# An attention and gated-MLP kernel on one core: identity made on the chip, shorter loads, and conversion steps given to GpSimd

## The chip, the cores and the metric

The kernel runs on 1 core of a Trainium2 chip. The metric is device time in microseconds (us), from the first to the last work of one execution. One execution was also recorded by the hardware profiler; views of that record are called the profile, or the trace where single instructions are meant.

A core has five engines that run side by side, each through its own instructions in a fixed order: PE (TensorE, matrix products), ACT (ScalarE), DVE (VectorE), POOL (GpSimd) and SP (SyncE, which here only issues DMA transfers). They wait for each other through semaphores. An engine whose next instruction waits does nothing else meanwhile.

## The reference, cut to what matters

```python
def phi(x):                       # x: batch 4, heads 4, 1088 positions, 32 channels
    a = np.einsum('rd,bhsd->bhsr', S1, x)        # r = 8
    b = np.einsum('rd,bhsd->bhsr', S2, x)
    return np.einsum('bhsi,bhsj->bhsij', a, b).reshape(*x.shape[:-1], 64)
q_p, k_p = phi(q), phi(k)
kv = np.einsum('bhsf,bhsd->bhfd', k_p, v)
num = np.einsum('bhsf,bhfd->bhsd', q_p, kv)
den = np.einsum('bhsf,bhf->bhs', q_p, k_p.sum(2))[..., None] + 1e-06
x = (num / den).transpose(0, 2, 1, 3).reshape(4, 1088, 128)

h = np.maximum(x @ w_in, 0.0)                    # 128 -> 1024
u, v = h[..., :512], h[..., 512:]
v_n = (v - mean(v)) / np.sqrt(var(v) + 1e-06)    # over the 512 channels
v_s = np.einsum('ts,bsd->btd', w_spatial, v_n) + b_spatial[None, :, None]
out = (u * v_s) @ w_out                          # 512 -> 128
```

`S1`, `S2`, `w_in` and `w_out` come in double precision (64 bits), the rest in single precision.

## The kernel before, in words

**Products.** Most products are made in three: each operand is split into a high part (ACT rounds it to the matmul's fast format) and a low part (what is left, a subtraction on DVE or POOL), and high x high, high x low and low x high are added up in PSUM (`mm3`, `high`, `low`). `wTh`/`wTl` are the two parts of `w_spatial`, `vh`/`vl` those of the normalised `v`, `wih`/`wil` and `woh`/`wol` those of `w_in` and `w_out`.

**Stages.** Batch 0 goes through `attention0`: keys and values of three groups of 384 positions are projected (`project`), expanded (`features`, tile `kp`), summed into `kv`, masked into `kd0` by a table of ones and zeros, then the queries of the three groups are expanded, transposed against an identity matrix `ident_sb`, multiplied (`sums`), divided, and transposed again into `xh`/`xl`. `hidden_v` makes the `v` half of the hidden layer in nine tiles of 128 positions, with the statistics of each row on DVE (`bn_stats`). `main` runs the spatial product. For batch 0 its first 424 columns are done for all four blocks of channels at once: first a high phase (36 pairs of matmuls against `wTh`, nine row tiles `kt` in order), then a low phase (36 matmuls against `wTl`). In between, `hidden` makes `u` (tile `pu`). Then follow the remaining columns, and the same for batches 1 to 3, whose attention is laid beside the main loop of the batch before. 

**Weights.** `w_in` is loaded in two halves (`load_wi`; half 1 serves `hidden_v`, half 0 serves `u`), `w_out` in one. Each is turned from 64 bits into 32 by `from_f64`: seven steps over 512 columns (absolute value, clamp, shift, sign, exponent, two more to add the lower word) and then the split. The small table `sk` (`S1`, `S2`) goes through the same steps over 64 columns, and nothing can be projected before it is ready. `load_w` loads `w_spatial` in 27 pieces (nine `kt`, three column ranges: `W0`, `W1`, `W2`).

**What sets the order.** `Order` holds every operation with its inputs, its outputs and an assumed cost, and `schedule` writes one order for each engine ahead of time, from tables of numbers: `LEADS`, `T_MAIN`, `PACE`, `STRETCH`, `SLACK`, `LEAD`, `FIRST`, and `FORCE`, which says which engines may take an operation. Where it expects PE to stand idle in the first 50 us it puts in short matmuls of no use (`fill`, L431), beside eight at the start (L427). On the chip each engine keeps its written order, whatever the real times are. In the kernel before, `FORCE` keeps the low parts `W0` and `W1` and the low parts of `v` of batch 0 (`vl0`) on DVE; all steps of `from_f64` but the absolute value are on DVE too.

**Loads.** All DMAs are issued by SP in order. `ident_sb` is loaded from the input `idn`: the identity in 128 columns, and two masks in 6 columns. A tile of the tag `pl` (8 buffers), `kt` or `v` (3 each) can be loaded again only after its last reader is done.

Of the kernel before, what the change touches and what calls it, by code (L numbers as in the profile page):

```python
# [9 lines left out]
F32 = mybir.dt.float32  # L10
# [4 lines left out]
ALU = mybir.AluOpType  # L15
# [4 lines left out]
P = 128  # L20
# [26 lines left out]
T_MAIN = (39.0, 143.0, 197.0, 292.0)  # L47
PACE = (1.145, 0.898, 1.306, 1.037)
STRETCH = 1.64
FORCE = {'abs': ['ACT'], 'norm0': ['ACT', 'DVE'], 'vl0': ['DVE'], 'v90': ['ACT'], 'W0': ['DVE'], 'W1': ['DVE'], 'W2': ['POOL']}  # L50

FIRST = ('wt21', 'wt20', 'wt02', 'wt12', 'wt11', 'wt40', 'wt01', 'wt22')
# [18 lines left out]
FIRST_RATE, LOW_DELAY = 0.18, 4.4  # L71
# [48 lines left out]
class Order:  # L120
# [13 lines left out]
    def op(self, eng, cost, fn, r=(), w=(), due=None, kb=0, alts=(), sh=False, kind=None, after=0.0, lead=0.0, f4=False):  # L134
# [208 lines left out]

def c_dve(n):
    return 152 + 1.045 * n


def c_dve2(n, ptr=False):
    return (270 if ptr else 155) + 0.53 * n


def c_pool(n):
    return 90 + 2.4 * n


def c_mm(n, k=1):
    return k * max((n + 11.8) / 2.25, 111)


@with_exitstack  # L360
def tile_kernel(ctx: ExitStack, tc: tile.TileContext, kT, qT, vA, sks, idn, wT, w_in, w_out, bsp, out):

# [85 lines left out]
    def from_f64(x32, raw, n):  # L448

        def w(i):
            return raw[:, :2 * n].bitcast(U32).rearrange("p (n w) -> p w n", w=2)[:, i]

        def x():
            return x32[:, :n]

        def xb():
            return x32[:, :n].bitcast(U32)

        def step(cost, f, r, w):
            op("DVE", cost, lambda: f(nc.vector), r=r, w=w, sh=True)

        c2, c1 = c_dve2(n), c_dve(n)

        if n > NSK:
            op("ACT", c_act(n), lambda: nc.scalar.activation(x(), w(1).bitcast(F32), AF.Abs), r=[raw], w=[(x32, "x")], sh=True, alts=[("DVE", c2, lambda: nc.vector.tensor_scalar(out=xb(), in0=w(1), scalar1=0x7FFFFFFF, scalar2=None, op0=ALU.bitwise_and))], kind="abs")
        else:
            step(c2, lambda v: v.tensor_scalar(out=xb(), in0=w(1), scalar1=0x7FFFFFFF, scalar2=None, op0=ALU.bitwise_and), [raw], [(x32, "x")])
        step(c2, lambda v: v.tensor_scalar(out=x(), in0=x(), scalar1=EXP_LO, scalar2=EXP_HI, op0=ALU.max, op1=ALU.min), [], [(x32, "x")])  # L470
# [9 lines left out]
        step(c1, lambda v: v.tensor_tensor(out=x(), in0=x(), in1=ev(), op=ALU.add), [(x32, "e")], [(x32, "x")])  # L480

    def split(hi, lo, x, n, r, wh, wl, pool=False, due=None, alt=False):

        op("ACT", c_act(n), lambda: nc.scalar.copy(out=hi(), in_=x()), r=r, w=wh)  # L484
        if pool:
            op("POOL", c_pool(n), sub_pool(lo, x, lambda: hi().bitcast(F32)), r=[*r, *wh], w=wl, due=due)
        else:
            alts = [("POOL", c_pool(n), sub_pool(lo, x, lambda: hi().bitcast(F32)))] if alt else []
            op("DVE", c_dve(n), sub(lo, x, lambda: hi().bitcast(F32)), r=[*r, *wh], w=wl, due=due, sh=True, alts=alts)
# [12 lines left out]
    wTh = tl(None, "wTh", [P, NS, S], F32R)  # L502
    wTl = tl(None, "wTl", [P, NS, S], F32R)
# [628 lines left out]
```

## Time and profile before

| | us |
|---|---|
| time, median of 3 runs (lowest to highest) | 335.46 (335.34 to 336.05) |
| the profiled execution's own time | 335.18 |
| its span in the profile | 333.4 |

The profiled execution's time holds 1.8 us that lie outside the span. Times in the views count from the span's start. A row of the timeline reads: start, length, engine, line of the kernel, operation, tile written <- tiles read, size, count, and in brackets the idle time before it and what ended that. An instruction's length runs from its start to its last write, so the next on the same engine often starts some 0.1 us before it ends.

### The profile page before, as it was taken

The numbers are of one execution on the slowest core, as the hardware profiler recorded it, in microseconds if no ns is written. First come the engines' busy times: TensorE is split into PE (matmuls) and PEld (weight loads), VectorE is DVE, ScalarE is ACT, GpSimd is POOL, SyncE is SP. The second block draws the span as 40 slices with busy tenths as digits, with TensorE's granted clock in tenths as the row PEclk, the third lists the DMA queues.
The fourth block names the chain that finished last, engine by engine and source line by source line (L and its number), as shares of the span: only waits on it lengthen the run. The fifth ranks groups of instructions, "written<-read, shape, count | busy, mean of one in ns | idle before, by whom it ended". The sixth has DMA issues, their size and how long they took to land.

```text
span 333.4 us, 6019 instructions
## 1 busy us (share of the span) xinstructions
PE 326.5 (98%) x2304; PEld 315.4 (95%) x2304; DVE 197.4 (59%) x448; ACT 157.9 (47%) x367; POOL 56.9 (17%) x68
## 2 busy tenths in 40 slices
PE   7999999999999999999999999999999999999996
PEld 7878979999999999999999999999999999999995
DVE  4899997355889972779984232255992473121221
ACT  2589667532668652556563232336651542121212
POOL 1000105472423106401313200131000000000000
PEclk9999999999999999999999999999999999999999
DMA  7901379667310175501037110310000100000001
GB/s 210 342 20 48 109 191 316 127 135 194 86 44 27 29 123 95 118 0 48 22 54 119 42 46 0 50 31 0 3 0 2 40 27 2 0 2 0 0 2 68
DMA packets 17747, 23.09 MB, mean 69 GB/s; under 512 B 2486, under 2 KB 17462, under 8 KB 17718
## 3 DMA queue, kind: packets, MB, share of 16 engines
q1 hardware_dynamic: 17718, 22.71, 27.0%
q8 instruction: 18, 0.29, 0.4%
q14 instruction: 11, 0.09, 0.1%
HBM read 13.78 MB, written 2.23 MB: 48 GB/s over the span
## 4 chain that ended last, share of the span: by engine, by line
PE 86%; DVE 7%; ACT 2%; DMA 2%; SPq 1%; issue 1%; DVEq 0%; ACTq 0%
PE sp L956 20%; PE sp L965 18%; PE sp L958 17%; PE sd L404 3%; PE sd L405 3%; PE sd L406 3%; PE pu L404 2%; PE po L405 2%; PE pu L406 2%; PE pu L405 2%; PE sp L967 2%; PE po L406 2%; PE po L404 2%; PE sd L614 2%; DMA v<-in_vA 2%; PE sd L568 1%
## 5 line engine op out<-in xcount | busy, mean ns | idle before, releaser
L956 PE MATMUL sp<-wTh,vh 128*128 128x362 f32 (+4 forms) x414 | 135.9, 328 | 0.0
L958 PE MATMUL sp<-wTh,vl 128*128 128x362 f32 (+4 forms) x368 | 120.4, 327 | 0.0
L965 PE MATMUL sp<-wTl,vh 128*128 128x362 f32 (+4 forms) x368 | 119.0, 328 | 0.7 <-DVE wTl L533 0.7
L956 PEld LDWEIGHTS sp<-wTh,vh 128*128 128x128 f32 x414 | 78.0, 188 | 1.0
L965 PEld LDWEIGHTS sp<-wTl,vh 128*128 128x128 f32 x368 | 69.3, 188 | 1.6 <-DVE wTl L533 1.3
L958 PEld LDWEIGHTS sp<-wTh,vl 128*128 128x128 f32 x368 | 69.4, 188 | 0.7
L993 DVE TENSOR_TENSOR u<-sp,u 128x362 f32<-128x362 f32 (+3 forms) x36 | 18.4, 510 | 45.1 <-PE sp L967 44.6
L484 ACT CAST g<-u 128x362 fp32r<-128x362 f32 (+3 forms) x34 | 16.4, 482 | 38.8 <-DVE u L993 38.6
L783 DVE RECIPROCAL c<-c 128x384 f32<-128x384 f32 (+1 forms) x9 | 21.7, 2416 | 10.5 <-ACT c L781 10.5
L417 POOL TENSOR_TENSOR r<-pl,r 128x384 fp32r<-128x384 f32 (+1 forms) x18 | 17.6, 982 | 59.1 <-ACT r L484 55.1
L809 DVE BATCH_NORM_STATS2 st<-vt 128x6 f32<-128x512 f32 x36 | 24.3, 689 | 4.9 <-ACT vt L807 4.8
L414 DVE TENSOR_TENSOR g<-u,g 128x362 fp32r<-128x362 f32 (+3 forms) x34 | 19.8, 581 | 11.0 <-ACT g L484 10.9
L807 ACT ACTIVATE vt<-sd 128x512 f32<-128x512 f32 x36 | 21.4, 600 | 9.1 <-PE sd L406 8.4
L749 POOL TENSOR_TENSOR pl<-pl,pl 128x384 f32<-128x384 f32 (+1 forms) x18 | 17.6, 984 | 35.7 <-DMA pl<-abT 32.0
L417 POOL TENSOR_TENSOR r<-c,r 128x384 fp32r<-128x384 f32 (+1 forms) x9 | 10.0, 1116 | 75.5 <-ACT r L484 75.5
L885 ACT CAST vh<-vt 128x384 fp32r<-128x384 f32 x36 | 17.2, 511 | 11.3 <-PE sp L956 4.9
L948 ACT ACTIVATE u<-pu 128x362 f32<-128x362 f32 (+3 forms) x36 | 16.4, 455 | 11.0 <-PE pu L406 10.8
L993 DVE TENSOR_TENSOR kp<-sp,kp 128x424 f32<-128x424 f32 x10 | 6.0, 600 | 26.1 <-PE sp L967 26.1
L887 DVE TENSOR_TENSOR vl<-vt,vh 128x384 fp32r<-128x384 f32 (+1 forms) x36 | 17.3, 504 | 1.4 <-ACT vh L885 1.3
L404 PE MATMUL pu<-xh,wih 128*128 128x362 f32 (+4 forms) x48 | 15.9, 331 | 0.0
L406 PE MATMUL pu<-xh,wil 128*128 128x362 f32 (+4 forms) x48 | 15.8, 329 | 0.0
L405 PE MATMUL pu<-xl,wih 128*128 128x362 f32 (+4 forms) x48 | 15.7, 328 | 0.0
(166 smaller groups left out, 540.2 us busy)
## 6 DMA issues: line engine op xcount, KB each, us to landing
pl<-in_wT SPq DMA_DIRECT2D x18, 166.0 KB, 3.7
v<-in_vA SPq DMA_DIRECT2D x12, 198.0 KB, 4.0
kt<-in_kT SPq DMA_DIRECT2D x12, 192.0 KB, 3.2
pl<-abT SPq DMA_DIRECT2D x12, 192.0 KB, 3.9
pl<-in_wT SPq DMA_DIRECT2D x9, 212.0 KB, 4.7
c<-in_qT SPq DMA_DIRECT2D x9, 192.0 KB, 2.8
pl<-abT SPq DMA_DIRECT2D x24, 72.0 KB, 2.3
pl<-abT SPq DMA_DIRECT2D x6, 160.0 KB, 3.7
```

Source lines behind the costliest of these rows:

```text
L404: nc.tensor.matmul(o, ah, bh, start=start, stop=False)
L405: nc.tensor.matmul(o, ah, bl, start=False, stop=False)
L406: nc.tensor.matmul(o, al, bh, start=False, stop=stop)
L414: return lambda: nc.vector.tensor_tensor(out=o(), in0=a(), in1=bb(), op=ALU.subtract)
L417: return lambda: nc.gpsimd.tensor_tensor(out=o(), in0=a(), in1=bb(), op=ALU.subtract)
L783: op("DVE", 135 + 6.3 * n, lambda x32=x32, n=n: nc.vector.reciprocal(out=x32[:, :n], in_=x32[:, :n]), w=[x32])
L807: op("ACT", c_act(512, True), lambda pv=pv, t=t: nc.scalar.activation(vt[:, t], pv.ap, AF.Relu), r=[pv], w=[(vt, t)])
L809: op("DVE", 690, lambda stats=stats, t=t: nc.vector.bn_stats(out=stats.ap, in_=vt[:, t]), r=[(vt, t)], w=[stats])
L956: nc.tensor.matmul(sp[:, :cw], vh[:, kt], wTh[:, kt, cs], start=(kt == 0), stop=False)
L958: nc.tensor.matmul(sp[:, :cw], vl[:, kt], wTh[:, kt, cs], start=False, stop=False)
L965: nc.tensor.matmul(sp[:, :cw], vh[:, kt], wTl[:, kt, cs], start=False, stop=False)
L993: op("DVE", c_dve(cw), lambda: nc.vector.tensor_tensor(out=u.ap, in0=sp[:, :cw], in1=u.ap, op=ALU.mult), r=[sp], w=[u], lead=LEAD[1])
```

## The change

- **Identity and masks on the chip.** The input `idn` and its DMA go. POOL writes ones into `ident_sb` and cuts all but the diagonal out with `affine_select`; it writes the mask `by_head` with three small memsets; DVE adds up columns of `ident_sb` to get the other mask, `in_turn`.
- **No padding loaded.** The third key group of batch 0 is loaded in 320 columns, not 384, and POOL clears the rest; the third query group of batch 0 is loaded in 320 columns, and POOL copies 64 columns behind them.
- **POOL may take single steps.** In `from_f64` the clamp and the last addition may go to POOL (`both`), so may the low parts of `w_in` and `w_out`. The table `FORCE` now names the engines for each operation singly (`W0.3`, `vl0.1`, `f64.wi_x1.6`, ...).
- **The order is set anew** by new values in all tables of numbers.

```diff
-T_MAIN = (39.0, 143.0, 197.0, 292.0)
-PACE = (1.145, 0.898, 1.306, 1.037)
-STRETCH = 1.64
+T_MAIN = (14.0, 136.0, 237.0, 300.0)
+PACE = (1.339, 0.8, 0.968, 0.88)
+STRETCH = 3.34
...
-FIRST = ('wt21', 'wt20', 'wt02', 'wt12', 'wt11', 'wt40', 'wt01', 'wt22')
+FIRST = ('wt42', 'wt11', 'wt21')
...
-LEAD = (8700, 7600)
+LEAD = (6100, 500)
...
-SLACK = {'PE': 5, 'ACT': 29, 'DVE': 91, 'POOL': 5000, 'SP': 5000}
+SLACK = {'PE': 7, 'ACT': 140, 'DVE': 55, 'POOL': 5000, 'SP': 2528}
...
-            o.alts = tuple(a for a in o.alts if a[0] in FORCE.get(kind, [eng]))
+            o.alts = tuple(a for a in o.alts if a[0] in FORCE.get(kind, FORCE.get(kind.split(".")[0], [eng])))
...
+        def step(cost, f, r, w, both=False):
+
+            steps.append(f)
+            alts, kind = [], None
+            if both and n > NSK:
+                alts, kind = [("POOL", c_pool(n) if cost == c1 else c_pool1(n), lambda: f(nc.gpsimd))], f"f64.{x32.name}.{len(steps)}"
+            op("DVE", cost, lambda: f(nc.vector), r=r, w=w, sh=True, alts=alts, kind=kind)
...
-    ident = tl(None, "ident_sb", [P, P + 6])
-    load(ident, lambda: ident.ap, idn, 70)
+    ident = tl(None, "ident_sb", [P, P])
+    op("POOL", 260, lambda: nc.gpsimd.memset(ident.ap, 1.0), w=[ident])
+    op("POOL", 400, lambda: nc.gpsimd.affine_select(out=ident.ap, in_=ident.ap, pattern=[[-1, P]], compare_op=ALU.is_equal, fill=0.0, base=0, channel_multiplier=1), w=[ident])
+    by_head = tl(None, "by_head", [P, 2, 2])
+    op("POOL", 120, lambda: nc.gpsimd.memset(by_head.ap, 0.0), w=[by_head])
+    for a in range(2):
+        op("POOL", 120, lambda a=a: nc.gpsimd.memset(by_head[64 * a:64 * a + 64, :, a], 1.0), w=[by_head])
+    in_turn = tl(None, "in_turn", [P, 2])
+    op("DVE", 290, lambda: nc.vector.tensor_reduce(
+        out=in_turn.ap, in_=ident.ap.rearrange("p (g a i) -> p a g i", a=2, i=R), axis=mybir.AxisListType.XY, op=ALU.add,
+    ), r=[ident], w=[in_turn])
...
-        load(xt, lambda: xt.ap, kT[b, g], 192, after=AFTER[b])
+        n = 384
+        if not b and g == 2:
+
+            n = 320
+            op("POOL", 240, lambda: nc.gpsimd.memset(xt[:, n:], 0.0), w=[(xt, 1)])
+        load(xt, lambda: xt[:, :n], kT[b, g, :, :n], n // 2, w=(xt, 0), after=AFTER[b])
```

The order that comes out differs almost everywhere; three places follow. Line numbers in the new kernel are higher by 5 to 30.

The first place is the start of POOL's order. Before (L441 are the constant ones that serve the bias; the `ISA` row is the instruction pair that loads POOL's code library, which `TENSOR_TENSOR` and `AFFINE_SELECT` on this engine call for):

```order
L441 CAST v_74<-z_67 64x128
L441 CAST v_78<-z_67 64x128
L441 CAST v_82<-z_67 64x128
L441 CAST v_84<-z_67 64x128
L417 ISA
L417 TENSOR_TENSOR r_660<-c_94,r_522 128x384
```

Now:

```order
L510 MEMSET ident_sb 128x128
L511 ISA
L511 AFFINE_SELECT ident_sb<-ident_sb 128x128
L513 MEMSET by_head 128x4
L515 MEMSET by_head 64x2 x2
L624 MEMSET kt 128x64
```

and, after four casts of those constants:

```order
L704 COPY c_128<-c_128 128x64
L492 TENSOR_TENSOR vt_216<-vt_216 128x512
L554 TENSOR_TENSOR wTl<-pl_209,wTh 128x424
L554 TENSOR_TENSOR wTl<-pl_209,wTh 128x332
L946 TENSOR_TENSOR vl<-vt_331,vh 128x512 x2
```

The library's loading has moved from behind the constants, ahead of work of a much later stage, to the front of the order, ahead of the identity; behind it stand now five steps that DVE had before (`vt_216` is `w_in`'s half 1 in conversion).

The second place is the start of DVE's order. Before (`z_67` is a constant for PE's first matmuls):

```order
L422 MEMSET z_67 128x128
L423 MEMSET z_67 2x128
L469 TENSOR_SCALAR sk<-pl_70 128x64
L470 TENSOR_SCALAR sk<-sk 128x64
L472 TENSOR_SCALAR sk<-sk 128x64
```

Now:

```order
L427 MEMSET z_69 128x128
L428 MEMSET z_69 2x128
L517 TENSOR_REDUCE in_turn<-ident_sb 128x2
L481 TENSOR_SCALAR sk<-pl_65 128x64
L482 TENSOR_SCALAR sk<-sk 128x64
```

The sum for `in_turn`, which reads the identity that POOL makes, stands ahead of the conversion of `sk`, and so ahead of everything else that DVE does.

The third place is PE's order at the end of `hidden_v` of batch 0, where the high phase begins (`sd` holds `hidden_v`, `pu` holds `u`, `sp` and `po` the spatial product). Before:

```order
L431 MATMUL po_111<-z_67 128x64 x10
L404 MATMUL sd_113<-wih,xh_290 128x512
L405 MATMUL sd_113<-wil,xh_290 128x512
L406 MATMUL sd_113<-wih,xl_294 128x512
L404 MATMUL sd_76<-wih,xh_290 128x512
L405 MATMUL sd_76<-wil,xh_290 128x512
L406 MATMUL sd_76<-wih,xl_294 128x512
```

Now:

```order
L436 MATMUL po_136<-z_69 128x64 x4
L409 MATMUL pu_146<-xh_292,wih 128x424
L410 MATMUL pu_146<-xl_303,wih 128x424
L411 MATMUL pu_146<-xh_292,wil 128x424
L436 MATMUL po_136<-z_69 128x64 x5
L409 MATMUL sd_118<-wih,xh_292 128x512
L410 MATMUL sd_118<-wil,xh_292 128x512
L411 MATMUL sd_118<-wih,xl_303 128x512
```

One `u` product stands now among the fill matmuls ahead of the last group of `hidden_v`, and two more inside the high phase; before, all four stood in and behind the low phase. For that, half 0 of `w_in` is converted before the last group, not after it.

More of the change, by code (lines that the diff above doesn't have):

```diff
@@ L360, in tile_kernel @@
 @with_exitstack
-def tile_kernel(ctx: ExitStack, tc: tile.TileContext, kT, qT, vA, sks, idn, wT, w_in, w_out, bsp, out):
+def tile_kernel(ctx: ExitStack, tc: tile.TileContext, kT, qT, vA, sks, wT, w_in, w_out, bsp, out):
     nc = tc.nc
@@ L515, in load_wi @@
         from_f64(x, raw, 512)
-        split(lambda: wih[:, sl], lambda: wil[:, sl], lambda: x[:, :512], 512, [(x, "x")], [(wih, (j, 0))], [(wil, (j, 0))])
+        split(lambda: wih[:, sl], lambda: wil[:, sl], lambda: x[:, :512], 512, [(x, "x")], [(wih, (j, 0))], [(wil, (j, 0))], alt=f"f64.wil{j}")
     def load_wo(raw, x):
@@ L533, in low @@
             return lambda: eng.tensor_tensor(out=wTl[:n, kt, cs], in0=raw[:n, :cw], in1=wTh[:n, kt, cs].bitcast(F32), op=ALU.subtract)
-        op("POOL", c_pool(cw), low(nc.gpsimd), r=[raw, (wTh, (kt, c))], w=[(wTl, (kt, c))], alts=[("DVE", c_dve(cw), low(nc.vector))], sh=True, kind=f"W{c}")
+        op("POOL", c_pool(cw), low(nc.gpsimd), r=[raw, (wTh, (kt, c))], w=[(wTl, (kt, c))], alts=[("DVE", c_dve(cw), low(nc.vector))], sh=True, kind=f"W{c}.{kt}")
     def load_bias():
@@ L673, in attention0 @@
             xt = tl("c", f"qt{b}{g}", [P, 384])
-            load(xt, lambda xt=xt, g=g: xt.ap, qT[b, g], 192)
+            n = TW[g]
+            load(xt, lambda xt=xt, n=n: xt[:, :n], qT[b, g, :, :n], n // 2, w=(xt, 0))
+            if n < 384:
+                op("POOL", 250, lambda xt=xt, n=n: nc.gpsimd.tensor_copy(out=xt[:, n:], in_=xt[:, n - 64:n]), r=[(xt, 0)], w=[(xt, 1)])
             qts.append(xt)
@@ L761, in part @@
                     src = v[:, :, D:].broadcast_to([P, 2, D]) if den else v[:, :, :D]
[L762 to L764 removed]
+                    nc.vector.tensor_tensor(out=kd[:, 1 + pr if den else 3 * pr], in0=src, in1=in_turn.ap.unsqueeze(2).broadcast_to([P, 2, D]), op=ALU.mult)
+                op("DVE", 215, part, r=[kv, in_turn], w=[(kd, (pr, den))])
         kvh, kvl = tl("kvh", f"kvh{b}", [P, 2, P], F32R), tl("kvl", f"kvl{b}", [P, 2, P], F32R)
@@ L916, in low @@
                     return lambda: eng.tensor_tensor(out=all_d(ls), in0=x(), in1=all_d(hs).bitcast(F32), op=ALU.subtract)
-                op("DVE", c_dve(DH), low(nc.vector), r=[(vt, t), *((h, kt) for h in hs)], w=[(l, kt) for l in ls], sh=True, alts=[("POOL", c_pool(DH), low(nc.gpsimd))], kind="vl0")
+                op("DVE", c_dve(DH), low(nc.vector), r=[(vt, t), *((h, kt) for h in hs)], w=[(l, kt) for l in ls], sh=True, alts=[("POOL", c_pool(DH), low(nc.gpsimd))], kind=f"vl0.{kt}")
             else:
```

40 lines of the change are left out of this document (19 added, 21 removed).

## The prediction

> **What bounds the kernel now.** First the head of the page, then the table of who waited for whom on PE, then the busy time by stages.
>
> ```profile
> span 333.4 us, 6019 instructions
> PE 326.5 (98%) x2304; PEld 315.4 (95%) x2304; DVE 197.4 (59%) x448; ACT 157.9 (47%) x367; POOL 56.9 (17%) x68
> ...
> PE sp L965 <- DVE wTl L533: 0.7, 1, 0.7
> PE sd L404 <- ACT vt L807: 0.5, 1, 0.5
> ...
> 20.00:30.00 10.00, 9.41 (x58) 7.66 (x58) 9.70 (x35) 8.82 (x20) 0.00 (x0) 1.00 0.14 41
> 40.00:50.00 10.00, 9.35 (x47) 8.31 (x47) 9.97 (x22) 6.18 (x15) 0.00 (x0) 1.00 0.65 178
> 250.00:300.00 50.00, 50.00 (x296) 49.09 (x295) 18.51 (x44) 14.71 (x35) 0.00 (x0) 1.00 0.04 12
> ```
>
> PE is the bound, at granted clock 1.00, and from about 54 us on it never pauses. In a stage row the columns are length, then busy time of PE, weight load, DVE, ACT, POOL, the clock, the DMA share and GB/s: at 250 us PE is busy 50.00 of 50, while in the first 50 us DVE is full (9.70 and 9.97 of 10) and POOL idle. The matmuls that the change keeps are the same ones, and the order at the very end (last gate, last products, three stores) is the same on each engine. So the time can change only by when PE gets through the start, unless the new order makes a wait later on. The start, in the timeline:
>
> ```profile
> 3.40 0.20 DVE L469 TENSOR_SCALAR sk<-pl 128x64 uint32<-128x64 uint32 x1 [2.13 <-DMA pl<-in_sks]
> ...
> 4.84 0.23 DVE L480 TENSOR_TENSOR sk<-sk 128x64 f32<-128x64 f32 x1
> 6.08 3.90 DVE L576 TENSOR_TENSOR kp<-ka,sd 128x768 f32<-128x768 f32 x4 [1.01 <-ACT ka L573]
> 10.72 0.30 DVE L665 TENSOR_TENSOR kd<-pu,ident_sb 128x132 f32<-128x132 f32 x1 [0.74 <-PE pu L614]
> ...
> 27.19 0.54 DVE L721 TENSOR_TENSOR xl<-sp,xh 128x384 fp32r<-128x384 f32 x1
> ...
> 25.27 2.34 PE L431 MATMUL po<-z 128*128 128x64 f32 x20
> 27.42 0.48 PE L404 MATMUL sd<-wih,xh 128*128 128x512 f32 x1
> ...
> 28.20 0.40 PE L404 MATMUL sd<-wih,xh 128*128 128x512 f32 x1
> 28.44 0.39 PE L405 MATMUL sd<-wil,xh 128*128 128x512 f32 x1
> ...
> 30.32 0.35 PE L956 MATMUL sp<-wTh,vh 128*128 128x424 f32 x1
> ...
> 46.08 1.30 PE L965 MATMUL po<-wTl,vh 128*128 128x424 f32 x6
> ...
> 54.34 0.31 PE L956 MATMUL sp<-wTh,vh 128*128 128x332 f32 x1
> ```
>
> The milestones are `sk` ready at 5.07, `kd0` begun at 10.72, the third `xl` done at 27.73, and the second column range begun at 54.34.
>
> **The change, part by part: the identity.** This decides. DVE's second task is now `in_turn`, which reads the identity, and DVE takes its work in order: `sk`, and with it all projections, waits until POOL has made it. POOL must first load its code library, which in the kernel before stands after the constants. What the trace shows of that loading:
>
> ```profile
> L417 POOLq EVENT_SEMAPHORE  x3: 17/43/12058, 26.4 to 38.6; - x3
> L417 POOLq MODIFY_POOL_CONFIG  x2: 18/18/18, 2.3 to 2.3; - x2
> ...
> 1.34 1.01 POOL L441 CAST v<-z 64x128 fp32r<-64x128 f32 x4 [0.90 <-DVE z L423]
> 38.60 1.01 POOL L417 TENSOR_TENSOR r<-c,r 128x384 fp32r<-128x384 f32 x1 [36.25 <-ACT r L484]
> ...
> 24.06 0.82 SPq L411 DMA_DIRECT2D c<-in_qT  x2
> ```
>
> Two configuration instructions of 18 ns at 2.3 us; then POOL does nothing until 38.60, when its input comes from ACT. How long the loading really took is hidden under that wait: from 0.04 us (the two instructions) up to 36.3 us. The semaphore row at 26.4 narrows nothing, since its first condition is a query load that SP issued at 24.06. The nearest rows are loads from memory in the same first microseconds:
>
> ```profile
> vt<-in_w_in SPq DMA_DIRECT2D x1, 512.0 KB, 6.0
> ...
> ident_sb<-in_idn SPq DMA_DIRECT2D x1, 67.0 KB, 3.4
> ```
>
> 67 KB took 3.4 us to land and 512 KB took 6.0 us. I take 6 us for the library, nearer to the larger one because it is a program for a whole engine; it is an estimate. Then: POOL is free at about 0.75 us, when the other engines begin; memset 0.3 (nearest, the casts, a quarter of 1.01); loading 6.0; `affine_select` 0.35 (a third of the 1.01 us for 384 columns); so the identity stands at 7.4 us. `in_turn` 0.3 (as L665), `sk` 1.67 (3.40 to 5.07), to the first `kp` 1.01, four `kp` 3.90, after which the last key sum has long its values: `kd0` at 14.3 instead of 10.72, **+3.6 us**. Were the loading free, the identity would be there at 1.5 us, before the table for `sk` (3.40), and nothing would wait.
>
> The Trainium skill (GPSIMD Engine Reference, 2.1 Instruction dispatch) speaks against this change: the first call into a freshly loaded kernel library pays about 6 us (5.95 measured) that no instruction in the profile shows. By it the term would be the same within 0.1 us; the trace here neither confirms nor denies it, since the wait covers it.
>
> **Shorter loads.** 67 KB for the identity, 32 KB of key padding and 32 KB of query padding are not loaded, and one issue (0.47 us on SP) goes ahead of the values. Now the third values tile ends a chain that starts before `kd0`:
>
> ```profile
> 4.50 5.13 DMA v<-in_vA
> ...
> 9.76 0.92 PE pu L614 x24
> ```
>
> It would land some 0.4 us earlier (99 KB at the 0.31 MB/us of this stretch is 0.3; issue 0.47). This counts only if the identity is early: then `kd0` is at 10.3, -0.4. If DVE starts late, the loads have long landed and it is worth nothing; it is not in the sum.
>
> **From `kd0` to the third `xl`.** DVE is full here, so I count its instructions (a bn_stats advances DVE by 0.60: 1.29 for two less the 0.69 of one).
>
> ```profile
> L809 DVE BATCH_NORM_STATS2 st<-vt 128x6 f32<-128x512 f32 x9 | 6.0, 687 | 0.0
> L480 DVE TENSOR_TENSOR v<-v 128x512 f32<-128x512 f32 x2 | 1.4, 681 | 0.0
> L470 DVE TENSOR_SCALAR v<-v 128x512 f32<-128x512 f32 x2 | 0.8, 414 | 0.0
> L533 DVE TENSOR_TENSOR wTl<-pl,wTh 128x424 fp32r<-128x424 f32 (+3 forms) x18 | 9.1, 536 | 0.0
> L845 DVE TENSOR_SCALAR vt<-vt,mv,sm 128x512 f32<-128x512 f32 x4 | 2.0, 533 | 0.0
> L916 DVE TENSOR_TENSOR vl<-vt,vh 128x512 fp32r<-128x512 f32 x8 | 5.4, 679 | 0.0
> ```
>
> With 0.09 off each for overlap: half 1 of `w_in` gains the absolute value (+0.4, from ACT) and loses the last addition to POOL (-0.6); half 0 of `w_in` is now converted entirely before the third `xl`, which before had got only as far as its third step there: two two-input steps, one one-input step and the split more (3 x 0.59 + 0.32, +2.1); one low part of `w_spatial` +0.5; a normalisation and two small steps less, -0.7. That is +1.7 of work, of which, by estimate, 0.5 falls into waits that DVE had in this stretch: **+1.2 us**.
>
> **From the third `xl` to the second column range.** Before, this took 27.42 to 54.34, 26.9 us. PE's own work in it: 116 matmuls of 424 columns at 0.19 (six in 1.30, of which the last takes 0.35) are 22.0, nine of 512 at 0.24 (28.20 to 28.44) are 2.2, three of 384 are 0.5 by their width: 24.7. So 2.2 us were lost, 0.5 and 0.7 of it in the two waits above, the rest in restarts and short gaps. In the new order one `u` product (three matmuls, 0.6) runs ahead, in the hole that 20 fill matmuls (2.34 us) filled; two low parts are ready before, two low parts of `v` and one of `W1` go to POOL. Counted from the third `xl`, DVE's new list up to the last low part of the first range is: seven low parts of `v` (4.2), three statistics (1.8), fifteen low parts of `w_spatial` (6.9), four normalisations (1.7, L845), three steps for `w_out` (1.4) and small ones (1.8), 17.8 us. PE asks for that part after the last `hidden_v` (2.2), 68 matmuls of the high phase (12.9), two `u` (1.2) and 18 of the low phase (3.4), 19.7 us: 1.9 us of slack where before there was a wait. **-2.8 us** (2.2 + 0.6).
>
> **What comes back.** DVE and POOL block each other:
>
> ```profile
> L925 DVE TENSOR_TENSOR vh<-vt,vh 64x512 fp32r<-64x512 f32 x1 | 1.4, 1398 | 0.0
> ...
> 50.47 1.83 DVE L533 TENSOR_TENSOR wTl<-pl,wTh 128x424 fp32r<-128x424 f32 x4
> ...
> 51.04 2.14 POOL L417 TENSOR_TENSOR r<-c,r 128x384 fp32r<-128x384 f32 x1 [11.42 <-ACT r L484]
> ```
>
> L925 began 0.17 us into POOL's 38.60 step and took 1.40 us, where such a subtraction (L916) takes 0.68; POOL's step at 51.04 took 2.14 instead of 1.01, ending 0.9 after DVE's run of low parts. The steps on POOL are laid beside statistics, which read one operand; the real times will not keep to that everywhere. One POOL step in the low phase is a clamp that DVE's `w_out` conversion waits for, and a query split stands behind it. Bounds: 0 (all beside statistics) to 3 us (six steps that each hold DVE for half of about 1 us). Since 1.9 us of it is slack, I take **+0.4**.
>
> **The sum.** +3.6 + 1.2 - 2.8 + 0.4 = +2.4 on the profiled execution's 335.18 (span 333.4 and 1.8 around it): 337.6. The median of the runs stands 0.28 above that execution: 337.9.
>
> **The rivals.**
>
> *The loading is free* (the library is still resident, or loads in well under 2 us). For: both instructions take 18 ns. Against: a code library has to come from somewhere, and no row shows POOL working soon after. Then -0.4 + 1.2 - 2.8 + 0.4 = -1.6: 333.9. This is the faster side; it decides where the identity stands before 3.4 us, so a loading under 2 us, and up to 3.5 us the gains still outweigh the delay. Chance 0.26.
>
> *The loading waits for the data stream.* The stages with their DMA share (second last column):
>
> ```profile
> 8.00:10.00 2.00, 1.65 (x58) 1.54 (x53) 1.88 (x2) 0.24 (x1) 0.00 (x0) 1.00 0.98 333
> 10.00:12.00 2.00, 1.90 (x42) 1.62 (x37) 0.63 (x2) 1.03 (x3) 0.00 (x0) 1.00 1.03 394
> 16.00:18.00 2.00, 2.00 (x19) 2.00 (x20) 2.00 (x4) 2.00 (x5) 0.00 (x0) 1.00 0.44 158
> ```
>
> The DMA engines are full until 16 us. In the new kernel SP runs on without DVE until it needs a buffer that only a projection frees: 2.7 MB, at 0.31 MB/us over by 10.7 us. Loaded only then, the library stands at 17, `kd0` begins at 24, +13.3 instead of +3.6: 347.6. Anything between 9 us of loading and this belongs here. Chance 0.23.
>
> *The loading is free, but POOL's lock eats the gain*: 2 us more than I took, PE stopped in the low phase: 335.9, from 334.8 to 336.2. The Trainium skill (SBUF — State Buffer, Who interferes with whom) calls the shared ports an exclusive lock for a whole instruction, against POOL's steps as well as DVE's two-input ones; by the two rows above the trace agrees. Chance 0.09.
>
> **How the numbers follow.** Forecast, loading of 4 to 9 us, 336 to 341: 0.42. With the rivals: faster by over 0.2% (0.67 us, about what a measurement of this kernel can tell from no change) 0.27, within it 0.06, slower 0.67. The range reaches from the free loading, of which the lower third is left out (333.6), to the long one, of which nearly half is left out (345.5).
>
> **What would show it.** In the new profile: the start of the `in_turn` sum on DVE (7.4 by my sum, under 2 if loading is free, 17 if it waits); PE's idle time between its first matmuls and the first projection; `kd0` at 14.3; no wait of PE on `wTl` in the low phase; DVE's third `xl` some 18 us behind `kd0` (before 17.0). The forecast is wrong if `in_turn` starts before the table of `sk` lands, or if PE waits again after 60 us, which nothing before it does.

## The result and the profile after

| | before | changed |
|---|---|---|
| median, us (lowest to highest, 6 runs each) | 335.47 (335.34 to 336.05) | 338.08 (336.25 to 338.63) |
| the profiled execution's own time | 335.18 | 336.79 |
| its span | 333.4 | 335.1 |

The ratio is 1.0062, with a 95% interval of 1.0036 to 1.0089: the changed kernel is slower by 0.6%. The forecast was 337.9. The number is close; the profile shows that the reason given for it is wrong. Medians below leave out two disturbed executions, one of a_best (895.44 us) and one of a_pick2 (534.66 us).

The head of the changed kernel's page, PE's table of waits, and the busy time by stages (columns as in the prediction):

```profile
span 335.1 us, 6007 instructions
PE 327.4 (98%) x2302; PEld 314.7 (94%) x2302; DVE 201.9 (60%) x450; ACT 158.4 (47%) x364; POOL 63.7 (19%) x77
...
PE sp L995 <- DMA pl<-in_wT: 1.7, 1, 1.7
...
20.00:30.00 10.00, 9.43 (x56) 7.21 (x56) 10.00 (x31) 8.37 (x19) 2.72 (x2) 1.00 0.54 161
40.00:50.00 10.00, 9.66 (x50) 9.05 (x49) 8.92 (x18) 7.88 (x20) 5.00 (x3) 1.00 0.63 172
50.00:60.00 10.00, 8.64 (x49) 8.53 (x50) 9.90 (x19) 6.88 (x16) 1.89 (x2) 1.00 0.79 220
```

In the kernel before, the last of these rows reads:

```profile
50.00:60.00 10.00, 10.00 (x59) 9.84 (x58) 7.45 (x14) 7.52 (x20) 5.72 (x5) 1.00 0.89 276
```

PE's largest wait is now one of 1.7 us in the low phase (L995; before 0.7), and between 40 and 60 us it is busy 18.30 of 20 (before 19.35). POOL now works from 20 to 30 and from 40 to 50 us, where it stood idle before. DVE is fuller than before from 20 to 30 and from 50 to 60 us, and less full from 40 to 50, where it waits. Next the start, in the timeline and in the answer on line 511:

```profile
L511 POOLq MODIFY_POOL_CONFIG  x2: 8/8/8, 0.9 to 1.0; - x2
...
0.80 0.20 POOL L510 MEMSET ident_sb<- 128x128 f32 x1 [0.29 <-POOLq L1149]
1.07 0.29 POOL L511 TENSOR_SCALAR_AFFINE_SELECT ident_sb<-ident_sb 128x128 f32<-128x128 f32 x1
...
1.40 0.29 DVE L517 TENSOR_REDUCE in_turn<-ident_sb 128x2 f32<-128x128 f32 x1
2.64 0.20 DVE L481 TENSOR_SCALAR sk<-pl 128x64 uint32<-128x64 uint32 x1 [0.95 <-DMA pl<-in_sks]
...
5.91 0.95 DVE L597 TENSOR_TENSOR kp<-ka,sd 128x768 f32<-128x768 f32 x1 [1.61 <-ACT ka L594]
...
10.58 0.30 DVE L691 TENSOR_TENSOR kd<-pu,by_head 128x132 f32<-128x132 f32 x1 [0.24 <-PE pu L640]
...
29.00 0.53 DVE L751 TENSOR_TENSOR xl<-sp,xh 128x384 fp32r<-128x384 f32 x1
```

`affine_select` runs at once behind the two configuration instructions, the identity is there at 1.4, and DVE then waits 0.95 us for the table of `sk`, not for POOL. Loading the library cost nothing that can be seen. `kd0` starts at 10.58 (before 10.72), the third `xl` at 29.00 (before 27.19). The low phase, in the timeline:

```profile
44.89 1.83 DVE L554 TENSOR_TENSOR wTl<-pl,wTh 128x332 fp32r<-128x332 f32 x3
45.13 2.55 POOL L482 TENSOR_SCALAR v<-v 128x512 f32<-128x512 f32 x1 [3.67 <-DMA pl<-in_wT]
47.71 1.24 DVE L484 TENSOR_SCALAR v<-v 128x512 uint32<-128x512 uint32 x1 [0.99 <-POOL v L482]
47.65 1.02 POOL L422 TENSOR_TENSOR r<-c,r 128x384 fp32r<-128x384 f32 x1
...
50.72 0.58 DVE L554 TENSOR_TENSOR wTl<-pl,wTh 128x424 fp32r<-128x424 f32 x1
...
48.74 0.92 PE L995 MATMUL sp<-wTl,vh 128*128 128x424 f32 x4
51.36 0.46 PE L995 MATMUL sp<-wTl,vh 128*128 128x424 f32 x1 [1.70 <-DMA pl<-in_wT]
...
56.56 0.32 PE L986 MATMUL sp<-wTh,vh 128*128 128x332 f32 x1
```

POOL's clamp of `w_out` (L482) takes 2.55 us beside DVE's low parts. DVE's next step for `w_out` (L484) waits 0.99 us for it, and then takes 1.24 us beside POOL's next step, where alone it takes 0.41. The low part of the eighth row block stands behind that on DVE; it ends at 51.30, and PE starts again at 51.36. (The row names a DMA as what ended the wait. That DMA's data had been cast long before; what came last is the low part.) The second column range starts at 56.56 (before 54.34), with one query product of 0.53 more ahead of it. 2.22 less 0.53 is the 1.7 us by which the span is longer; behind it PE stands still for 0.05 us in all up to 300 us.

Most of the rest of the 2.6 us goes with the granted clock. Of the six runs two stand at a clock of 0.998 and 1.000 and take 336.79 and 336.25, four at 0.993 and 0.994 and take 338.02 to 338.63. The profile is of one of the first two.

### The profile page after: what moved, and what is told of

Read it like the earlier page. It is cut to its first block, busy times and chain, and to the rows that moved or that the text cites. A ratio compares the mean times of both kernels' runs of the same rounds, so it can differ in the third digit from the quotient of the medians.

```text
span 335.1 us, 6007 instructions
## 1 busy us (share of the span) xinstructions
PE 327.4 (98%) x2302; PEld 314.7 (94%) x2302; DVE 201.9 (60%) x450; ACT 158.4 (47%) x364; POOL 63.7 (19%) x77
## 4 chain that ended last, share of the span: by engine, by line
PE 78%; DVE 10%; DMA 4%; ACT 3%; issue 2%; SPq 1%; DVEq 0%; ACTq 0%
PE sp L986 18%; PE sp L995 16%; PE sp L988 16%; PE sd L409 3%; PE sd L410 3%; PE sd L411 3%; DMA pl<-in_wT 3%; PE po L410 2%; PE po L411 2%; PE sp L997 2%; PE po L409 2%; PE pu L409 2%; PE pu L411 2%; PE pu L410 2%; PE sd L640 2%
## 5 line engine op out<-in xcount | busy, mean ns | idle before, releaser
L995 PE MATMUL sp<-wTl,vh 128*128 128x362 f32 (+4 forms) x368 | 118.4, 327 | 1.7 <-DMA pl<-in_wT 1.7
L995 PEld LDWEIGHTS sp<-wTl,vh 128*128 128x128 f32 x368 | 69.3, 188 | 2.5 <-DVE wTl L554 2.0
L419 DVE TENSOR_TENSOR g<-u,g 128x362 fp32r<-128x362 f32 (+3 forms) x34 | 18.8, 552 | 11.5 <-ACT g L496 10.9
L917 DVE TENSOR_TENSOR vl<-vt,vh 128x384 fp32r<-128x384 f32 (+1 forms) x36 | 18.7, 533 | 3.3 <-ACT vh L915 3.1
L875 DVE TENSOR_SCALAR vt<-vt,mv,sm 128x512 f32<-128x512 f32 x31 | 15.4, 539 | 0.0
```

The source lines that it names most:

```text
L419: return lambda: nc.vector.tensor_tensor(out=o(), in0=a(), in1=bb(), op=ALU.subtract)
L917: return lambda: eng.tensor_tensor(out=vl[:, kk:kk + n], in0=x()[:, :n], in1=vh[:, kk:kk + n].bitcast(F32), op=ALU.subtract)
L995: nc.tensor.matmul(sp[:, :cw], vh[:, kt], wTl[:, kt, cs], start=False, stop=False)
```

## The experiments

All edits leave the tables of numbers alone. Those of the changed kernel act on the finished order, so that every other instruction keeps its place; b_ident and b_pad put their instructions in the places of the loads that they replace. Theory A: POOL's clamp holds DVE, and so stops PE. Theory B: the other new POOL steps cost DVE by the lock what they save. Theory C: PE's stop is what lowers the granted clock. In the names, `wTl:8` is the low part that PE waits for, `wo_x:2` the clamp, `wo_x:3` the step behind it. Medians are of 12 runs unless said; "before" is the kernel before on the same chip, 335.50 to 335.70, and each ratio is to it. The runs were spread over four chips, so where two edited kernels stood on different chips their ratios compare better than their medians.

**One instruction moved (a_low8_first).**

```diff
     order = k.schedule()
+    at = [getattr(o, 'name', None) for o in order]
+    o = order.pop(at.index('wTl:8'))
+    at = [getattr(x, 'name', None) for x in order]
+    order.insert(at.index('wo_x:3'), o)
```

> The changed kernel with one instruction moved: DVE makes the low part of the eighth row block of the first column range (the one that PE waits 1.70 us for) ahead of the w_out step that waits for POOL's clamp. Theory A (the clamp on POOL holds DVE, and what stands behind the held step stops PE): PE's stop of 1.70 us in the low phase is gone, the second column range begins at 54.9 instead of 56.56, the span is 333.4 instead of 335.1, 335.1 us in a run at a clock of 0.998 and more. Rival (DVE is simply full there): a stop of about the same length appears at the next low part or at the second column range, and the span stays within 0.4 of 335.1. On the clock: if the lower granted clock (0.993 in four of six runs of the changed kernel) follows from PE's stop, no run falls under 0.998 here; if it doesn't, runs at 0.993 still come, 1.6 us longer.

335.85, ratio 0.9997 (0.9985 to 1.0009); all clocks 0.999 or 1.000. The second column range starts at 55.24 and the span is 333.8, somewhat later than expected (54.9 and 333.4). PE's stop is gone, but another, shorter one has come. The timeline:

```profile
44.51 2.55 POOL L482 TENSOR_SCALAR v<-v 128x512 f32<-128x512 f32 x1 [3.67 <-DMA pl<-in_wT]
...
50.99 0.47 ACT L551 CAST wTh<-pl 128x332 fp32r<-128x332 f32 x1 [1.48 <-DMA pl<-in_wT]
...
53.15 0.51 ACT L496 CAST r<-c 128x384 fp32r<-128x384 f32 x1
...
53.73 1.00 POOL L422 TENSOR_TENSOR r<-c,r 128x384 fp32r<-128x384 f32 x1 [5.68 <-ACT r L496]
...
54.79 0.44 PE L410 MATMUL sd<-r,sqh 128*128 128x384 f32 x1 [0.63 <-POOL r L422]
```

PE now waits 0.63 us for POOL's second query split. POOL had stood idle for 5.68 us ahead of it: the split waits for ACT's cast `r`, and this cast stands behind casts of `w_spatial` that wait for their loads. DVE still waits 0.48 us for the clamp, and with the clamp on DVE (the next run) that cast begins at 51.78 and not at 53.15; that the clamp is what delays it, by way of DVE and the buffers that it frees, is argued from these two times. Theory A stands for the stop; no stop of about the same length has come in its place, as the rival of a full DVE had it.

**The clamp on DVE (a_clamp_dve).**

```diff
+        o.all = {a[0]: a[2] for a in o.alts}
...
     order = k.schedule()
+    for o in order:
+        if not isinstance(o, Fill) and o.name in {'wo_x:2': 'DVE'}:
+            o.eng = {'wo_x:2': 'DVE'}[o.name]
+            o.fn = o.all[o.eng]
```

> The changed kernel with the clamp of w_out on DVE instead of POOL, at the same place. Theory A: DVE pays 0.33 us for it and is freed of the 0.99 us wait and of some 0.8 us by which its step beside POOL was drawn out; PE's low part is there 1.5 us earlier, the stop falls from 1.70 to about 0.2, the span to 333.6. Rival (DVE is full): the stop stays over 1 us and the span over 334.5.

335.25, ratio 0.9985 (0.9970 to 0.9999), clocks 0.998 to 1.000; third `xl` at 28.42, second column range at 54.87, span 333.3. Giving one step of 0.41 us back to DVE takes the whole slowdown away. A wait of 0.56 us is left at the same place, more than the 0.2 expected. (0.6 of the 1.8 us by which this span is shorter lie ahead of the third `xl`, where the clamp plays no part; see a_again.) The same timeline shows the lock at its plainest:

```profile
42.04 5.24 POOL L423 TENSOR_TENSOR r<-c,r 128x384 fp32r<-128x384 f32 x1 [1.16 <-ACT r L497]
...
46.39 2.08 DVE L555 TENSOR_TENSOR wTl<-pl,wTh 128x332 fp32r<-128x332 f32 x3
...
49.64 0.46 PE L996 MATMUL sp<-wTl,vh 128*128 128x424 f32 x1 [0.56 <-DMA pl<-in_wT]
```

A subtraction that takes POOL 1.0 us elsewhere is 5.24 us on its way beside a run of DVE's subtractions with three one-tensor steps among them, and the DVE group that it ends in takes 2.08 instead of 1.32.

**All six new POOL steps on DVE (a_pool_off).**

```diff
-        if not isinstance(o, Fill) and o.name in {'wo_x:2': 'DVE'}:
+        if not isinstance(o, Fill) and o.name in {'wo_x:2': 'DVE', 'wi_x1:7': 'DVE', 'wTl:4': 'DVE', 'wTl:12': 'DVE', 'vl00:2': 'DVE', 'vl00:3': 'DVE'}:
```

> The changed kernel with all six of its new POOL steps on DVE at their places (last addition of w_in half 1, two low parts of w_spatial, two low parts of v, the clamp of w_out). DVE has 3.1 us more to do. If POOL's steps cost by the lock what they save (theory B): the third xl comes about 1.0 us later than 29.0, DVE's stalls beside POOL (24.74, 31.46, 33.26, 47.71; 2.5 us in all) are gone, and the span is 334.5 to 335.5. If they are a real relief of DVE and only the clamp is badly placed: PE waits 1.5 to 3 us more in the first 56 us and the span is 336.0 to 337.5.

335.39, ratio 0.9981 (0.9968 to 0.9994), third `xl` at 29.53, span 334.0, which is under both ranges expected (334.5 and more). Five POOL steps, 2.8 us of DVE's work, are worth 0.14 us beside the run above: theory B holds for the sum of them. The milestones show that it does not hold for each. Without the five steps the third `xl` is 1.1 later (29.53 against 28.42), but from there to the second column range it takes 0.5 less (25.97 against 26.45).

**The kernel before with the identity on chip (b_ident).**

```diff
-    load(ident, lambda: ident.ap, idn, 70)
+    op("SP", 470, on_chip, w=[ident], kb=70)
```

Here `on_chip` writes the identity and the masks with the changed kernel's instructions.

> The kernel before with its own order, only the identity and the masks made on chip instead of loaded (67 KB less; paddings still loaded). By the prediction's term (a first code loading of 6 us): the in_turn sum on DVE starts at 7.4, kd0 at 14.3, the time is 3.6 us longer, 338.8. By the trace of the changed kernel (the loading is free): in_turn starts before 1.5, kd0 at 10.3 to 10.7, and the time is 0 to 0.4 us shorter, 334.8 to 335.2 on the profiled execution.

334.50, ratio 0.9959 (0.9942 to 0.9976). In the timeline:

```profile
2.77 0.29 POOL L503 TENSOR_SCALAR_AFFINE_SELECT ident_sb<-ident_sb 128x128 f32<-128x128 f32 x1
...
3.10 0.29 DVE L507 TENSOR_REDUCE in_turn<-ident_sb 128x2 f32<-128x128 f32 x1 [1.75 <-POOL by_head L504]
...
10.84 0.30 DVE L678 TENSOR_TENSOR kd<-pu,by_head 128x132 f32<-128x132 f32 x1 [0.26 <-PE pu L627]
11.05 0.42 DVE L470 TENSOR_SCALAR vt<-vt 128x512 f32<-128x512 f32 x1
...
26.82 0.54 DVE L734 TENSOR_TENSOR xl<-sp,xh 128x384 fp32r<-128x384 f32 x1
```

In the kernel before, the conversion of `w_in` starts so:

```profile
11.66 0.43 DVE L470 TENSOR_SCALAR vt<-vt 128x512 f32<-128x512 f32 x1 [0.64 <-ACT vt L467]
```

The prediction's term is refuted: `in_turn` starts at 3.10 and not at 7.4 (it stands behind POOL's four casts here; my "before 1.5" missed that). `kd0` is no earlier; the gain begins at `w_in`, which lands sooner, so that its conversion starts at 11.05 and not at 11.66. That makes the third `xl` 0.37 earlier and the span 0.4 shorter. The medians differ by 1.1; what the other 0.7 are, these traces don't show.

**No padding either (b_pad).** The third key group and the third query group of the kernel above are loaded in 320 columns.

```diff
-            load(xt, lambda xt=xt, g=g: xt.ap, qT[b, g], 192)
...
+                n = TW[g]
+                nc.sync.dma_start(out=xt[:, :n], in_=qT[b, g, :, :n])
+                if n < 384:
+                    nc.gpsimd.tensor_copy(out=xt[:, n:], in_=xt[:, n - 64:n])
```

> The kernel before with the identity on chip and, in addition, no padding loaded (32 KB of keys and 32 KB of queries less; POOL fills the rest). If the early data stream is what the identity's gain came from, at 0.31 MB/us 64 KB are 0.2 us, and of that only the keys' half stands ahead of the values: 0.1 to 0.2 us less than with the identity alone (334.50), so 334.3. Rival: kd0 no longer hangs on the stream, and it is the same, 334.4 to 334.6.

334.40, ratio 0.9976 (0.9963 to 0.9988). Not to be told from the run above: the padding is worth nothing that 12 runs show.

**The changed kernel once more (a_again).**

> The changed kernel itself once more, unedited, for two questions. First, its distance to the same kernel with the clamp on DVE (335.25): by theory A (the clamp) 1.5 to 1.9 us, so 336.8 to 337.2. Second, the clock: four of its six first runs had a granted clock of 0.993 and took 338.0 to 338.6. If that belongs to this kernel (PE's stop), runs at 0.993 come again and make the median about 338; if it was the state of that chip in that hour, all runs here stand at 0.998 to 1.000 and the median is 336.3 to 337.0.

336.21 (336.06 to 338.21), ratio 1.0034 (1.0018 to 1.0050). Nine runs have a clock of 0.998 to 1.000 and take 336.06 to 336.98; three have 0.993 or 0.994 and take 337.77 to 338.21. With the first six, 7 of 18 runs of this kernel are low in the clock, and cost some 1.9 us more. In the two kernels without the 1.70 us stop above it is none of 24; of 98 runs of the kernel before on these chips two stood at 0.995 (336.84 and 336.93). The new trace has the same stop of 1.7 us and the third `xl` at 28.37; the first had lost 0.6 us on the way to it, where the first `xh` came late from ACT, which had waited 1.07 us for a load (here 0.20).

The distance to the kernel with the clamp on DVE is 0.96 us by the medians and 1.2 by the profiled spans, not the 1.5 to 1.9 that theory A asked for: the 0.6 just named had been counted to the clamp. As for the clock, the recorded value alone proves no loss: one run of a_pool_off shows 0.950 and takes 335.29, no more than the others.

**Two POOL steps kept (a_pool_pick).**

```diff
-        if not isinstance(o, Fill) and o.name in {'wo_x:2': 'DVE'}:
+        if not isinstance(o, Fill) and o.name in {'wo_x:2': 'DVE', 'wTl:12': 'DVE', 'vl00:2': 'DVE', 'vl00:3': 'DVE'}:
```

> The changed kernel with only two of its six new POOL steps left on POOL, the two that DVE's statistics and small steps run beside (last addition of w_in half 1, low part of the fourth row block); the second column range's low part, both low parts of v and the clamp on DVE. In the changed kernel DVE lost 0.7 beside the first of these (the step at 24.74 took 0.85, alone 0.15) and 1.7 beside the two low parts of v (1.27 and 0.74 for steps of 0.15), where the work itself costs DVE 0.42 and 1.2. If POOL's steps cost DVE what the lock rows say: 0.3 less to the third xl and 0.5 less after it, 334.5 to 335.0. Rival (five POOL steps are worth nothing either way, as with all off): 335.2 to 335.4.

334.48 (8 runs), ratio 0.9970 (0.9957 to 0.9982): 0.8 under the kernel with five POOL steps and 0.9 under that with none. (Both stood on another chip; by the ratios it is 0.5 and 0.4, and the intervals overlap.) The milestones are plainer: the third `xl` at 28.36, as early as with the five steps, and from there to the second column range 25.98, as short as with none. The changed kernel's timeline shows what went:

```profile
24.29 1.29 POOL L554 TENSOR_TENSOR wTl<-pl,wTh 128x332 fp32r<-128x332 f32 x1 [2.85 <-ACT wTh L551]
24.74 0.85 DVE L866 SCALAR_TENSOR_TENSOR sm<-mv,sm 128x3 f32<-128x3 f32 x1
...
31.19 2.79 POOL L946 TENSOR_TENSOR vl<-vt,vh 128x512 fp32r<-128x512 f32 x2 [5.61 <-ACT vh L943]
31.46 1.27 DVE L866 SCALAR_TENSOR_TENSOR sm<-sm,sm 128x3 f32<-128x3 f32 x1
...
33.26 0.74 DVE L866 SCALAR_TENSOR_TENSOR sm<-sm,sm 128x3 f32<-128x3 f32 x1
```

In the kernel with two steps the same instruction reads:

```profile
30.84 0.15 DVE L867 SCALAR_TENSOR_TENSOR sm<-sm,sm 128x3 f32<-128x3 f32 x1
```

An instruction over three columns, but with two tensors to read, is held by POOL, by 1.12 us here and by 0.70 at 24.74; the statistics beside it aren't. Two tensors alone are not enough. In the changed kernel's timeline stands also:

```profile
14.93 1.28 POOL L492 TENSOR_TENSOR vt<-vt 128x512 f32<-128x512 f32 x1 [3.10 <-DVE vt L491]
...
15.22 0.94 DVE L597 TENSOR_TENSOR kp<-ka,sd 128x768 f32<-128x768 f32 x1
```

This DVE instruction takes 0.94 us beside POOL's, and 0.95 alone (5.91 above). One of its two tensors, `sd`, lies in PSUM, where the matmuls write; the ones that were held read both from SBUF, the memory of all other tiles.

**A low part put off, with a load and a cast (a_best).** Four moves on the kernel above, with the four lines of a_low8_first for each (what, ahead of what; `wt80:1` is the load, `wTh:9` the cast):

```diff
+    move=[('wTl:8', 'wo_x:3'), ('wTl:6', 'st020:1'), ('wt80:1', 'qt10:1'), ('wTh:9', 'vt01:5')]
```

> The kernel of the run before this one, with one low part of the first column range (the sixth row block, which stands 10 us ahead of the third xl on DVE though PE asks for it only in the low phase) moved behind the third xl, together with the load that takes its buffer next and the cast of that load; and with the eighth row block's low part ahead of the w_out step. If the third xl sets when the high phase begins, as the prediction's sum had it: the third xl 0.45 earlier and the time 0.4 to 0.5 less than with the two POOL steps alone. Rival (DVE is full up to the low phase, so what is put off comes back there): PE waits on wTl in the low phase by as much, and the time stays within 0.15.

335.02 (11 runs), ratio 0.9979 (0.9964 to 0.9993), from 334.00 to 335.65. By the medians it is 0.5 slower than without the moves (the intervals overlap), so neither expectation was met. The profiled execution is the one left out, so no trace says why; a moved load is what only this kernel has.

**A longer stop on purpose (a_stop_long).** On the changed kernel, the moves written as above:

```diff
+    move=[('wo_x:5', 'wTl:8'), ('wTl:14', 'wTl:8'), ('wo_x:6', 'wTl:8'), ('wo_x:7', 'wTl:8')]
```

> The changed kernel with PE's stop in the low phase made longer on purpose: four DVE instructions that PE isn't waiting for (2.2 us in all) go ahead of the low part that it does wait for. By the work alone the stop goes from 1.70 to 3.9 us, and the time from 336.2 to 338.4. Theory C (PE's stop is what lowers the granted clock, in 7 of 18 runs of the changed kernel and in none of the other kernels, whose stops are 0.7 and less): a longer stop does it in nearly every run, and each then shows a clock of 0.994 or less and 1.6 us more, 340.0, with a stretch of about 3 us at half clock in the profile right behind the stop. Rival (the clock has to do with something else in that kernel): the share of runs at 0.993 and 0.994 stays near 0.4, and the others take 338.4.

340.78 (339.95 to 341.32, 4 runs), ratio 1.0153 (1.0135 to 1.0172). All four runs are low: clocks 0.993, 0.994, 0.989, 0.989. Stage rows of its profile (the clock is the third column from the end), and PE's timeline:

```profile
53.00:54.00 1.00, 1.00 (x5) 0.96 (x6) 0.26 (x1) 0.86 (x2) 0.59 (x1) 0.96 0.17 28
54.00:55.00 1.00, 1.00 (x4) 0.94 (x3) 0.00 (x0) 0.00 (x0) 0.42 (x1) 0.50 0.89 256
55.00:56.00 1.00, 1.00 (x4) 0.93 (x4) 0.33 (x1) 0.47 (x1) 0.00 (x0) 0.50 1.05 327
56.00:57.00 1.00, 1.00 (x4) 0.93 (x4) 1.00 (x3) 0.19 (x1) 0.00 (x0) 0.50 0.77 237
57.00:58.00 1.00, 1.00 (x6) 0.96 (x5) 0.98 (x3) 0.35 (x1) 0.00 (x0) 0.83 0.23 82
...
48.05 0.92 PE L995 MATMUL sp<-wTl,vh 128*128 128x424 f32 x4
52.90 0.46 PE L995 MATMUL sp<-wTl,vh 128*128 128x424 f32 x1 [3.93 <-DVE wTl L554]
...
55.43 2.58 PE L995 MATMUL po<-wTl,vh 128*128 128x424 f32 x8
```

Two of the four took 339.95 and 340.32 at 0.993 and 0.994, close to the 340.0 expected; the two at 0.989 took 1 us more, and have no trace. In the trace, 1.0 us after PE has started again the clock falls to half. What the five rows lack of 1.00 adds up to 1.71 us lost, which is 3.4 us at half clock; eight matmuls take 2.58 us there, where seven took 1.49 before the stop. Theory C holds for a stop of 3.9 us. That the runs of the changed kernel at 0.993 have such a stretch behind their 1.70 us is argued from the same clock and the same loss; no trace of such a run was had.

**A wait of the kernel before taken away (b_best).** On b_ident:

```diff
+    move=[('wTl:6', 'wil:2')]
```

> The kernel before with the identity on chip, and one low part of the first column range (sixth row block, which PE waits 0.65 us for at 45.42) ahead of w_in's last low part on DVE. If that wait is on the path: 0.5 to 0.65 less than 334.50, so 333.9. Rival (DVE is full, and the next low part comes late instead): 334.4 to 334.6.

335.29, ratio 0.9991 (0.9982 to 1.0001): 0.8 slower than b_ident. The wait for `wTl` is gone, and in its place stands another, as the timeline shows:

```profile
47.59 0.47 ACT L543 CAST wTh<-pl 128x332 fp32r<-128x332 f32 x1 [0.53 <-DMA pl<-in_wT]
47.96 0.52 ACT L961 ACTIVATE kp<-pu 128x424 f32<-128x424 f32 x1
...
48.53 0.46 PE L404 MATMUL pu<-xh,wih 128*128 128x424 f32 x1 [0.97 <-ACT kp L961]
```

ACT must read a `u` product out before PE can make the next, and stands at casts of `w_spatial` that wait for their loads. b_pad's profiled execution, the slowest of its 12, has the same wait, so it can come without the edit too. This one is the slowest of its 12 as well, and had already lost 0.96 us at the third `xl` (27.78 against 26.82), ahead of the moved instruction, where ACT waited 2.10 us for a load. What the 0.8 between the medians is stays open.

**The third `xl` earlier (a_pick2, a_pick3).** Edits on a_pool_pick; `sq:2`, `sq:1` and `sql:1` (DVE) and the cast `sqh:1` (ACT) build the query matrix.

```diff
+    move=[('sq:2', 'mv02:1'), ('sq:1', 'mv02:1'), ('sqh:1', 'vt02:3'), ('sql:1', 'st021:1'), ('wTl:8', 'wo_x:3')]
```

> The changed kernel with two new POOL steps only (334.48), and the four instructions that build the query matrix (0.45 us of DVE, asked for by PE only at 54 us) moved behind the third xl; the eighth row block's low part ahead of the w_out step. No buffer and no load changes its place this time. If the third xl sets the start of the high phase: it starts 0.4 earlier and the time is 334.1. Rival (what is put off comes back before the low phase's end): a wait of PE on wTl, and 334.4 to 334.6.

334.17 (7 runs), ratio 0.9961 (0.9946 to 0.9976). In this kernel the cast stood ahead of the copies whose result it reads, so the high part of the query matrix holds other numbers; the instructions are the same. With the cast behind them:

```diff
-('sqh:1', 'vt02:3'), ('sql:1', 'st021:1')
+('sqh:1', 'vt01:4'), ('sql:1', 'mv02:3')
```

> As the run before this one, but with the cast that makes the high part of the query matrix put behind the two copies that fill the matrix (in that run it stood ahead of them, and so the query matrix' high part was formed from what the buffer held earlier). Same instructions on the same engines. If the third xl sets the high phase: third xl at 27.5 to 28.0, the high phase from 29.2 to 29.6, no wait of PE on wTl, and 334.0 to 334.4, 0.3 to 0.5% under the kernel before. Rival (the order of that run, with ACT's cast free of a wait, was what made it quick): 334.5 to 334.8.

334.16 (8 runs, 333.82 to 334.67), ratio 0.9963 (0.9951 to 0.9975): faster than both kernels. In its timeline:

```profile
27.61 0.55 DVE L752 TENSOR_TENSOR xl<-sp,xh 128x384 fp32r<-128x384 f32 x1
...
29.23 0.36 PE L987 MATMUL sp<-wTh,vh 128*128 128x424 f32 x1
...
53.59 0.32 PE L987 MATMUL sp<-wTh,vh 128*128 128x332 f32 x1
```

Against a_pool_pick the third `xl`, the high phase and the second column range are all 0.75 earlier, the span 0.7 shorter, and no wait on `wTl` has come. In these two executions the third `xl` does set what follows it. The medians differ by only 0.3, and a_pick3's profiled execution is the fastest of its eight, so the size of the gain is less sure than its place.

## Why the number was right and the reasons were not

By its own steps, on the profiled execution:

| step | forecast | measured | how |
|---|---|---|---|
| to `kd0` (identity) | +3.6 | -0.14 | 10.58 against 10.72 |
| `kd0` to third `xl` | +1.2 | +1.95 | 18.42 against 16.47 |
| third `xl` to second column range | -2.8 | -0.12 | 27.56 less 0.53, against 27.15 |
| POOL's lock coming back | +0.4 | in the row above | |
| sum | +2.4 | +1.7 | |
| median over the profiled execution | +0.28 | +1.29 | 338.08 less 336.79 |

- **The identity: wrong.** The step that failed is "I take 6 us for the library". The trace had bounded the loading from 0.04 to 36 us, and I priced it by the nearest loads from memory. Both new traces (the changed kernel and b_ident) show two instructions, of 8 and of 10 ns, and `affine_select` right behind. The Trainium skill (GPSIMD Engine Reference, 2.1 Instruction dispatch) has about 6 us for a first call into a freshly loaded library; this trace disagrees, with at most the 0.07 us between the memset's end at 1.00 and the start at 1.07. Whether the library was freshly loaded here, or still there from an execution before, no run shows. `in_turn` stands ahead of the table of `sk`, which the prediction itself had named as a sign of being wrong. The rival of a free loading was right in its condition (of its 0.4 us for an earlier `kd0` 0.14 came), and the identity alone makes the kernel before faster.
- **To the third `xl`: right.** 1.95 in the first trace, and 1.3 in the second (10.58 to 28.37), where ACT didn't hold the first `xl`; the forecast was 1.2.
- **From the third `xl`: the gain is there and was given back.** With the lock's worst steps removed (a_pool_pick), 28.36 to 54.34 less 0.53 is 25.45, 1.7 under the kernel before; 2.8 was too much.
- **The lock: the term that was mis-sized.** Taken at 0.4, bounded by 3. The changed kernel's rows add up to 4.2 us of DVE: 0.70 beside the low part at 24.29 (a step of 0.15 took 0.85), 1.71 beside those of `v` (1.12 and 0.59), 1.82 at the clamp (0.99 of wait, 0.83 of stretching). These four steps took 2.0 us of work off DVE (0.42, 1.2 and 0.33). L484, the step stretched at the clamp, reads one tensor only and was held all the same. The 1.9 us of slack for the last low part, and with it "no wait of PE on wTl in the low phase", weren't there. The clamp was named as the place, and not priced.
- **The clock: not in the sum at all.** 7 of 18 runs pay some 1.9 us more behind the stop; of the first six it was four, and they make the median. That the stop is the cause is shown for 3.93 us and argued for 1.70.

The total came out by luck: +3.6 that didn't come stood in for 2.3 us of gain that didn't last, 0.75 on the way to the third `xl` and 1.0 us of clock. The rival "the loading is free, but POOL's lock eats the gain", at 0.09, is what happened in kind; but it said 335.9, from 334.8 to 336.2, and the profiled execution took 336.8, the median 338.1. In the second measurement, with fewer runs low in the clock, the same kernel is slower by 0.34%.

## What to carry to other kernels

A step given to POOL is worth what DVE does beside it. The two steps kept in a_pool_pick, which ran beside statistics and a step that reads from PSUM, were a gain. Beside DVE instructions that read two tensors from SBUF, a POOL step cost more than it saved in both places (0.70 for 0.42, and 1.71 for 1.2). The clamp, whose result DVE itself needs next, was paid for twice, by the wait and by the next step's stretching. An order that leaves PE a stop can cost more than the stop, since the clock may follow. An unknown cost whose bounds are 0 and 36 us is a case of its own, not a term of the sum; here a right total hid wrong terms, and only the milestones told them apart.

## What the runs showed of the hardware

- A stop of PE of 3.93 us is followed, 1.0 us after the restart, by 3.4 us at half clock; one trace shows it, and all four runs have low clocks (0.989 to 0.994). With a stop of 1.70 us, 7 of 18 runs show 0.993 or 0.994. The Trainium skill (TensorE: Matmul & The Clock Gate, Part 1: The HAM clock gate) has the clock halved after an idle window of about 3.4 us, in windows that run freely. The slow stretch is as long as such a window. The rest doesn't agree: a stop of 3.93 us holds a whole window of 3.4 in about one case of six (an estimate from that page's figure: 0.5 of room in 3.4), and all four runs were low; a stop of 1.70 us never holds one. That a window idle for a part of it is enough, and that free windows explain why only some runs are low, is argued and not shown.
- The lock can starve POOL as well: 5.24 us for a subtraction that takes 1.0, beside a run of DVE's steps, most of them two-tensor subtractions.
- The first use of POOL's code library in an execution can be free: `affine_select` starts 0.07 us behind the instruction ahead of it.
- Beside a POOL step that reads from SBUF, a DVE instruction that reads one tensor from PSUM and one from SBUF was not held (0.94 us, alone 0.95); one over three columns that reads two from SBUF was (1.27 us, alone 0.15).
